# Retention attention with a multiplicative FFN in fp32: order of the first loads, and Strassen products in place of plain ones

## The chip, the cores and the metric

The kernel runs on one NeuronCore of a Trainium2 chip, in a single launch. The metric is the device time of that launch in microseconds (us): 935.48 as the median of nine runs. TensorE (PE) multiplies matrices, VectorE (DVE), ScalarE (ACT) and GpSimd (POOL) work elementwise, and SyncE (SP) issues nearly all the transfers. Each engine works through its own queue in order and meets the others at semaphores.

## The reference

Retention (attention with a decay in place of a softmax) on 8 batches, 8 heads, 576 positions and 64 dimensions gives x, 4608 tokens by 512. Then a feed-forward block multiplies two projections and projects twice:

```python
scores = scale * np.matmul(q, k.transpose(0, 1, 3, 2))
Dmat = np.where(rel >= 0, gamma[:, None, None] ** rel[None, :, :], 0.0)
ret = scores * Dmat[None, :, :, :]
attn = np.matmul(ret, v)
x = attn.transpose(0, 2, 1, 3).reshape(B * S, H * D)
a = x @ w1            # 512 x 1024
b = x @ w2            # 512 x 1024
h = a * b @ w3        # 1024 x 1024
out = h @ w_out       # 1024 x 512
```

q, k, v are float32. The four weights reach the chip as 64-bit floats and are turned into float32 there.

## The kernel before

**Attention.** The batches are taken in four pairs. The 576 positions of a pair are cut into five chunks, the first of 64 and four of 128; a chunk of a pair is called a unit here, so units 0 to 4 are the first pair. For unit g, `load(g, names)` (L95) issues one transfer of 512 KB for each of k, q and v (256 KB for unit 0; two buffers each), `scale` (L158, POOL) multiplies q and v by their decays, `front` (L166) transposes k and q on TensorE with copies on ScalarE, `score` (L183) multiplies them and masks the result into `pm` on VectorE (one buffer), `state` (L199) adds k and v to a running state, and `pv` (L220) multiplies `pm` by v, adds what the state gives, and copies the result into `xT`. A unit's `pv` needs its `score` and the earlier units' `state`.

**Weights.** w1 and w2 are cut into four quarters of columns, `fp` 0 to 3, of four blocks each (512 KB; w1 and w2, two halves of rows), blocks 0 to 15; w_out and w3 follow, 24 blocks more. `load_block` (L261) issues the next block into one of five `raw` buffers; a block whose second index is 1 goes as two transfers. They are numbered raw0, raw1 and so on here. The conversion from 64 bits is a generator: `begin_block` (L295) has three steps on VectorE and two activations on ScalarE, `end_block` (L320) two steps on VectorE, the last writing the block into `wA` and issuing the next load. The order is begin 0, begin 1, end 0, begin 2, end 1 and so on: block n is ended only after block n + 1 was begun. `convert(n)` takes n steps of it at the place where it is called, and `convert_up_to(n)` as many as n blocks need. Nothing reorders these steps later: the order of the calls is the order of the queues.

**Products with w1 and w2.** Tokens of a pair are taken in three parts n of 192 per batch, and `up(i, n, fp)` (L431) multiplies part n of pair i by quarter fp of w1 and w2 with Strassen's scheme: 7 products in place of 8. It needs four sums of each quarter, which `strassen_weights(fp)` (L146) makes from `wA` (S1, S2, S3, S4; S3 in place of a quarter's block), and three sums of tokens T, which `strassen_tokens(i, n)` (L397) makes, the fourth in place in `xT`. The results pass through VectorE additions into a tile `c` (one buffer), and two halves of `c` are multiplied into `ab`. `up_plain` (L413) does the same with 8 products, straight from `wA` and `xT`, with no sums: on TensorE it issues 64 instructions where `up` issues 56. It serves pair 0, part 0, quarters 0 and 1. The order of the start is written out by hand from L501 to L553; behind it, w3 times w_out is folded into one matrix (L563 to L580), and the rest of the kernel alternates attention of the later pairs, `up`, and `down` (L475).

What matters for the order: an engine's instructions stand in its queue as the calls below come. `convert` puts work on VectorE and ScalarE and loads on SP; `front` and `pv` put copies on ScalarE; `score`, `up` and the two `strassen_` functions put work on VectorE.

Of the kernel before, what the change touches and what calls it, by code (L numbers as in the profile page):

```python
# [8 lines left out]
F32 = mybir.dt.float32  # L9
# [23 lines left out]
def kernel(  # L33
# [13 lines left out]
    nc = tc.nc  # L47
# [6 lines left out]
    P = 128  # L54
# [10 lines left out]
    TB = S // NB  # L65
    NT = 2 * TB // P
    KD = DM // P
    KF = DF // P
# [6 lines left out]
    ffn = ctx.enter_context(tc.tile_pool(name="ffn", bufs=2))  # L75
# [12 lines left out]
    acc = ctx.enter_context(tc.tile_pool(name="acc", bufs=7, space=PSUM))  # L88
# [4 lines left out]
    live = {}  # L93

    def load(g, names, engine=nc.sync):  # L95
        i, c = divmod(g, NC)
        sz = sizes[c]
        src = {"k": k, "q": q, "v": v}
        for nm in names:
            t = pools["ld"].tile([P, 2 * H, D], F32, tag="ld_" + nm, name="ld_" + nm)  # L100
            engine.dma_start(  # L101
                t[:sz], src[nm][2 * i:2 * i + 2, :, starts[c]:starts[c] + sz, :].rearrange("b h p d -> p (b h) d"))
            live[nm, g] = t
# [34 lines left out]
    def A(fp, nm):  # L138

        h, m = divmod(fp, 2)  # L140
        if nm in ("S1", "S2", "S4"):
            return wS[h][:, ("S1", "S2", "S4").index(nm), m]
        r, f = {"A11": (0, 0), "A12": (1, 0), "A21": (0, 1), "S3": (0, 1), "A22": (1, 1)}[nm]
        return wA[h][:, :, 2 * r:2 * r + 2, m * QC + f * P:m * QC + f * P + P]

    def strassen_weights(fp):  # L146
        def tt(out, in0, in1, op):
            nc.vector.tensor_tensor(out=A(fp, out), in0=A(fp, in0), in1=A(fp, in1), op=op)  # L148

        tt("S1", "A21", "A22", ALU.add)  # L150
        tt("S2", "S1", "A11", ALU.subtract)
        yield
        tt("S3", "A11", "A21", ALU.subtract)
        tt("S4", "A12", "S2", ALU.subtract)
        live["S", fp] = True
        yield

    def scale(g, nm):  # L158
        c = g % NC
        sz = sizes[c]  # L160
        t, gam = live[nm, g], {"q": gq, "v": gk}[nm]
        t = t[:sz].rearrange("p (b h) d -> p b h d", b=2)
        nc.gpsimd.tensor_tensor(  # L163
            out=t, in0=t, in1=gam[:sz, c].unsqueeze(1).unsqueeze(3).to_broadcast([sz, 2, H, D]), op=ALU.mult)

    def front(g):  # L166
        c = g % NC
        sz = sizes[c]
        kn, qn = live["k", g], live["q", g]
        kT = pools["fr"].tile([P, 2, NP, P], F32, tag="kT", name="kT", bufs=1)  # L170
        qT = pools["fr"].tile([P, 2, NP, P], F32, tag="qT", name="qT")
        for src, dst in ((kn, kT), (qn, qT)):
            for b in range(2):
                tp = acc.tile([P, NP, P], F32, tag="acc", name="tp")
                for p in range(NP):
                    h = b * H + 2 * p
                    nc.tensor.transpose(tp[:, p, :sz],  # L177
                                        src[:sz, h:h + 2, :].rearrange("p a d -> p (a d)"),
                                        ident[:sz, :sz])
                nc.scalar.copy(dst[:, b, :, :sz], tp[:, :, :sz])  # L180
        live["kT", g], live["qT", g] = kT, qT

    def score(g):  # L183
        c = g % NC
        sz = sizes[c]
        kT, qT = live["kT", g], live["qT", g]
        pm = pools["fr"].tile([P, 2, 2, NP, P], F32, tag="pm", name="pm", bufs=1)
        for b in range(2):
            sc = [acc.tile([P, NP, P], F32, tag="acc", name="sc") for j in range(2)]
            for p in range(NP):  # L190
                for j, hs in enumerate(heads):
                    nc.tensor.matmul(sc[j][:sz, p, :sz], kT[hs, b, p, :sz], qT[hs, b, p, :sz],  # L192
                                     start=True, stop=True)
            for j in range(2):
                nc.vector.tensor_mul(pm[:sz, b, j, :, :sz], sc[j][:sz, :, :sz],  # L195
                                     mask[:sz, :sz].unsqueeze(1).to_broadcast([sz, NP, sz]))
        live["pm", g] = pm

    def state(g):  # L199
        c = g % NC  # L200
        sz = sizes[c]
        if c == NC - 1:
            return
        kn, vs = live["k", g], live["v", g]
        if c == 0:
            live["st"] = st_ps.tile([P, 2, NP, D], F32, tag="st", name="st")
        st = live["st"]

        for b in range(2):
            for p in range(NP):  # L210
                for j, hs in enumerate(heads):
                    h = b * H + 2 * p + j
                    nc.tensor.matmul(st[hs, b, p, :], kn[:sz, h, :], vs[:sz, h, :],  # L213
                                     start=(c == 0 and b == 0 and p == 0), stop=(c == NC - 2),
                                     skip_group_check=True)
        sb = pools["fr"].tile([P, 2, NP, D], F32, tag="sb", name="sb")
        nc.scalar.copy(sb, st)
        live["sb", g + 1] = sb
# [101 lines left out]
    def end_block():  # L320
        n = converted[0]
        hi = live["raw", n][:, :, 1]
        e, m = live["em", n]
        vec = nc.vector
        vec.scalar_tensor_tensor(e, in0=hi, scalar=-(1 << 31), in1=e,
                                 op0=ALU.bitwise_and, op1=ALU.bitwise_or)
        yield
        key = blocks[n][0]
        while not (key[0] == "w12" or "wo" in live and (key[0] == "wo" or key[1] < turned[0] + 2)):
            yield "wait"  # L330
        out, m, e = converted_to(n), m.bitcast(F32), e.bitcast(F32)
        if key[0] == "w12":
            m, e = (x.rearrange("p (c n) -> p c n", c=2) for x in (m, e))
        vec.scalar_tensor_tensor(out, in0=m, scalar=2.0 ** -20, in1=e, op0=ALU.mult, op1=ALU.mult)
        converted[0] += 1

        if n > 0:
            load_block()
        if key[0] == "w12" and key[1] > 1 and key[2:] == (1, 1):
            yield from strassen_weights(key[1])  # L340
        yield

# [18 lines left out]
    def convert(n):  # L361

        for _ in range(n):
            if go_on() is not None:
                return

    def convert_up_to(n):
        while converted[0] < n:
            assert go_on() is None
# [40 lines left out]
        minus(B[0][1], B[1][1], B[0][1])  # L410
        minus(T[2], B[1][0], T[1])

    def up_plain(i, n, fp, conv):  # L413

        convert_up_to(4 * (fp + 1))
        if fp == 0:
            live["ab", i, n] = ffn.tile([P, 2 * KF, TB], F32, tag="ab", name="ab")
        ab, x = live["ab", i, n], live["xT", i]
        c = ffn.tile([P, 4, 2, TB], F32, tag="c", name="c", bufs=1)
        for m, (a, b) in enumerate((a, b) for a in range(2) for b in range(2)):  # L420
            ps = acc.tile([P, 2, TB], F32, tag="acc", name="up")
            for w in range(2):
                for r in range(KD):
                    nc.tensor.matmul(ps[:, w, :], A(fp, f"A{a + 1}{r // 2 + 1}")[:, w, r % 2, :],  # L424
                                     x[:, r, b, n * TB:(n + 1) * TB], start=(w == r == 0),
                                     stop=(r == KD - 1), skip_group_check=True)
            nc.scalar.copy(c[:, m, 0], ps[:, 0, :])
            nc.vector.tensor_mul(ab[:, 4 * fp + m, :], ps[:, 1, :], c[:, m, 0])
            convert(conv)

    def up(i, n, fp, conv=0):  # L431
        m = every.index((i, n))
        while ("S", fp) not in live:
# [64 lines left out]
            nc.sync.dma_start(*stores.pop(0))  # L498


    load(1, "kqv")  # L501
    for _ in range(4):
        load_block()
    load(2, "kq")
    load_block()
    scale(0, "q")
    front(0)
    score(0)
    scale(0, "v")
    state(0)  # L510
    scale(1, "q")
    front(1)
    scale(1, "v")
    pv(0)
    load(2, "v")
    state(1)
    convert(3)
    score(1)
    convert(10)
    scale(2, "q")  # L520
    scale(2, "v")
    pv(1)
    load(3, "kq")
    load(3, "v")
    up_plain(0, 0, 0, conv=3)
    front(2)
    state(2)
    score(2)
    convert(5)
    load(4, "kq")  # L530
    scale(3, "q")
    scale(3, "v")
    front(3)
    pv(2)
    load(4, "v")
    state(3)
    score(3)
    up_plain(0, 0, 1, conv=3)
    pv(3)
    for _ in strassen_weights(0):  # L540
        pass
    strassen_tokens(0, 1, nc.vector)
    converting.append(strassen_weights(1))
    scale(4, "q")
    scale(4, "v")
    up(0, 1, 0, conv=2)
    front(4)
    up(0, 1, 1, conv=2)
    score(4)
    strassen_tokens(0, 0, nc.vector)  # L550
    up(0, 0, 2, conv=2)
    pv(4)
    att_part.close()  # L553
# [130 lines left out]
```

## Time and profile before

| | us |
|---|---|
| median of nine runs (lowest, highest) | 935.48 (931.17, 937.22) |
| profiled execution, its own time | 931.17 |
| its span, first to last instruction | 929.4 |
| PE busy | 903.1 (97%) |
| PE weight loads busy | 716.6 (77%) |
| DVE busy | 341.4 (37%) |
| ACT busy | 203.8 (22%) |
| POOL busy | 117.9 (13%) |
| idle of PE ahead of the plain products, 24.47 to 28.38 | 3.91 |
| idle of PE in the plain product, 33.29 to 36.07 | 2.78 |
| idle of PE ahead of the second plain quarter, 62.93 to 64.39 | 1.46 |
| idle of PE in `up(0, 0, 2)`, 102.14 to 106.55 | 4.41 |

The profile is of one execution. Its page cuts the span into 40 slices of 23.2 us, with a digit for the busy tenths of each engine and one for the clock that TensorE was granted. The chain of waits follows the last instruction back to what released it, step by step: each line has a start, a length and what it was. Timeline rows have a start, a length, the engine (with q: its queue, as for issues of transfers), the line, the operation, tiles out and in with their shapes, and in brackets how long the engine sat idle before and what released it. The fp32 products of this kernel show as two matmul instructions each.

### The profile page before, as it was taken

The numbers are of one execution on the slowest core, as the hardware profiler recorded it, in microseconds if no ns is written. First come the engines' busy times: TensorE is split into PE (matmuls) and PEld (weight loads), VectorE is DVE, ScalarE is ACT, GpSimd is POOL, SyncE is SP. The second block draws the span as 40 slices with busy tenths as digits, with TensorE's granted clock in tenths as the row PEclk, the third lists the DMA queues.
The fourth block names the chain that finished last, engine by engine and source line by source line (L and its number), as shares of the span: only waits on it lengthen the run. The fifth ranks groups of instructions, "written<-read, shape, count | busy, mean of one in ns | idle before, by whom it ended". The sixth has DMA issues, their size and how long they took to land.

```text
span 929.4 us, 14132 instructions
## 1 busy us (share of the span) xinstructions
PE 903.1 (97%) x6101; PEld 716.6 (77%) x6101; DVE 341.4 (37%) x593; ACT 203.8 (22%) x377; POOL 117.9 (13%) x87
## 2 busy tenths in 40 slices
PE   6689899999999999999999999999999999999998
PEld 6688799944456779959968959949959959689593
DVE  2679888885001213403313312403313304224040
ACT  3353233345112321111121111111211110011010
POOL 3220020000302423103003020003020101000000
PEclk9799899999999999999999999999999999999999
DMA  9983223342516652303024012134010010000101
GB/s 195 214 195 91 68 71 111 114 127 52 91 49 125 126 110 39 69 23 80 1 48 75 15 46 57 24 68 80 1 46 12 1 35 1 12 23 1 35 1 34
DMA packets 125550, 59.67 MB, mean 64 GB/s; under 512 B 113704, under 2 KB 113704, under 8 KB 125488
## 3 DMA queue, kind: packets, MB, share of 16 engines
q1 hardware_dynamic: 123824, 58.47, 28.2%
q8 instruction: 48, 0.79, 0.4%
q10 hardware_dynamic: 1664, 0.30, 0.2%
q14 instruction: 14, 0.11, 0.0%
HBM read 49.32 MB, written 9.44 MB: 63 GB/s over the span
## 4 chain that ended last, share of the span: by engine, by line
PE 91%; DVE 4%; DMA 2%; SPq 2%; issue 1%; ACT 0%; POOL 0%; DVEq 0%
PE up L448 44%; PE po L479 27%; PE ps L387 6%; PE sc L192 3%; PE xps L241 3%; PE tp L177 3%; SPq L101 2%; PE xps L234 2%; PE up L424 1%; DMA raw<-in_moe_w_dram 1%; PE st L213 1%; DMA ld_v<-in_v_dram 1%; PE tp L377 1%; DVE wS L148 1%; DVE pm L195 1%
## 5 line engine op out<-in xcount | busy, mean ns | idle before, releaser
L453 DVE TENSOR_TENSOR c<-up,c 128x384 f32<-128x384 f32 x230 | 127.9, 556 | 337.6 <-PE up L448 335.9
L479 PE MATMUL po<-w3o,ab 128*128 128x512 f32 x576 | 251.0, 593 | 0.0
L479 PEld LDWEIGHTS po<-w3o,ab 128*128 128x128 f32 x576 | 108.2, 190 | 129.2 <-issue 128.4
L448 PE MATMUL up<-xT,wA 128*128 128x192 f32 x1104 | 204.3, 328 | 0.5 <-ACT xT L245 0.5
L448 PEld LDWEIGHTS up<-xT,wA 128*128 128x128 f32 x1104 | 183.7, 191 | 4.2 <-issue 2.4
L448 PE MATMUL up<-T,wS 128*128 128x192 f32 x736 | 136.6, 329 | 5.3 <-DVE T L404 5.3
L448 PEld LDWEIGHTS up<-T,wS 128*128 128x128 f32 x736 | 123.7, 192 | 5.9 <-issue 4.7
L195 DVE TENSOR_TENSOR pm<-sc,mask 128x512 f32<-128x512 f32 (+1 forms) x80 | 45.4, 628 | 189.6 <-PE sc L192 189.6
L482 ACT COPY ot<-po 128x512 f32<-128x512 f32 x36 | 21.1, 586 | 238.6 <-PE po L479 238.6
L466 ACT COPY c<-up 128x384 f32<-128x384 f32 x46 | 22.0, 478 | 224.9 <-PE up L448 224.8
L163 POOL TENSOR_TENSOR ld_v<-ld_v,gk 128x1024 f32<-128x1024 f32 (+1 forms) x20 | 38.1, 1906 | 257.1 <-DMA ld_v<-in_v_dram 249.8
L163 POOL TENSOR_TENSOR ld_q<-ld_q,gq 128x1024 f32<-128x1024 f32 (+1 forms) x20 | 38.2, 1908 | 245.3 <-DMA ld_q<-in_q_dram 144.6
L448 PE MATMUL up<-xT,wS 128*128 128x192 f32 x368 | 67.7, 327 | 0.2 <-DVE c L453 0.2
L448 PE MATMUL up<-T,wA 128*128 128x192 f32 x368 | 67.3, 326 | 0.0
L448 PEld LDWEIGHTS up<-xT,wS 128*128 128x128 f32 x368 | 60.8, 190 | 1.2 <-DVE c L453 1.1
L448 PEld LDWEIGHTS up<-T,wA 128*128 128x128 f32 x368 | 61.1, 190 | 0.0
L387 PE MATMUL ps<-wo,w3T 128*128 128x512 f32 x128 | 56.3, 592 | 0.0
L472 DVE TENSOR_TENSOR ab<-c 128x768 f32<-128x768 f32 x46 | 44.0, 956 | 3.8
L387 PEld LDWEIGHTS ps<-wo,w3T 128*128 128x128 f32 x128 | 23.7, 190 | 26.8 <-issue 26.8
L459 ACT COPY c<-up 128x384 f32<-128x384 f32 x46 | 22.0, 478 | 84.0 <-DVE ab L472 58.0
L314 ACT ACTIVATE e<-e,lim 128x512 int32<-128x512 int32 x40 | 28.9, 722 | 52.3 <-DVE e L304 52.3
L192 PE MATMUL sc<-qT,kT 64*128 64x128 f32 (+1 forms) x640 | 38.5, 271 | 1.0 <-ACT qT L180 1.0
(55 smaller groups left out, 612.9 us busy)
## 6 DMA issues: line engine op xcount, KB each, us to landing
raw<-in_moe_w_dram SPq DMA_DIRECT2D x24, 512.0 KB, 3.7
ld_k<-in_k_dram SPq DMA_DIRECT2D x16, 512.0 KB, 6.3
ld_q<-in_q_dram SPq DMA_DIRECT2D x16, 512.0 KB, 7.4
ld_v<-in_v_dram SPq DMA_DIRECT2D x16, 512.0 KB, 4.6
out_dram<-ot SPq DMA_DIRECT2D x24, 256.0 KB, 2.0
raw<-in_moe_w_dram SPq DMA_DIRECT2D x16, 256.0 KB, 5.8
raw<-in_moe_w_out_dram SPq DMA_DIRECT2D x8, 512.0 KB, 3.5
out_dram<-ot SPq DMA_DIRECT2D x24, 128.0 KB, 2.3
```

What stands on the lines that cost most here:

```text
L163: nc.gpsimd.tensor_tensor(out=t, in0=t, in1=gam[:sz, c].unsqueeze(1).unsqueeze(3).to_broadcast([sz, 2, H, D]), op=ALU.mult)
L177: nc.tensor.transpose(tp[:, p, :sz], src[:sz, h:h + 2, :].rearrange("p a d -> p (a d)"), ident[:sz, :sz])
L192: nc.tensor.matmul(sc[j][:sz, p, :sz], kT[hs, b, p, :sz], qT[hs, b, p, :sz], start=True, stop=True)
L195: nc.vector.tensor_mul(pm[:sz, b, j, :, :sz], sc[j][:sz, :, :sz], mask[:sz, :sz].unsqueeze(1).to_broadcast([sz, NP, sz]))
L241: nc.tensor.matmul(banks[r][heads[half], b, n, :sz], vs[:sz, b * H + 2 * p + j, :], pm[:sz, b, j, p, :sz], start=(c == 0 and m == 0), stop ...
L314: nc.scalar.activation(e, e, relu, bias=lim[:, 0:1], scale=-1.0)
L387: nc.tensor.matmul(ps, live["w3T", ft][:, g, :], live["wo"][:, g, :], start=(g == 0), stop=(g == KF - 1))
L448: nc.tensor.matmul(ps[:, w, :], a[:, w, r, :], b[:, r, :], start=(new and w == r == 0), stop=(w == r == 1), skip_group_check=True)
L453: nc.vector.tensor_add(c[:, to], ps, c[:, sb])
L459: nc.scalar.copy(c[:, 0], p1)
L472: nc.vector.tensor_mul(ab[:, 4 * fp:4 * fp + 4, :], c[:, :, 0, :], c[:, :, 1, :])
L479: nc.tensor.matmul(po, ab[:, f, t * P:(t + 1) * P], live["w3o"][:, f, :], start=(f == 0), stop=(f == KF - 1))
```

## The change

The order written out by hand at the start of the kernel is another one, and `up_plain` is gone.

- Blocks 0 to 3 are issued ahead of k, q and v of unit 1, block 4 behind them; before, unit 1 went first, and unit 2's k and q between blocks 3 and 4.
- Conversion begins between `front(0)` and `score(0)`; `pv(0)` comes directly after more of it; quarter 0 is converted and its four sums are made ahead of `front(1)`. Blocks 5 to 7 are issued ahead of k, q and v of unit 2.
- `strassen_tokens(0, 0)` comes directly behind `pv(1)` and no longer behind `score(4)`.
- `up(0, 0, 0)` and `up(0, 0, 1)` take the place of the two plain products, the second ahead of `front(2)` and no longer behind `score(3)`.
- The sums of quarter 1 are made as part of its conversion, when its last block is ended, and no longer inside `up(0, 1, 0)`.
- Units 2 and 3 go through `front`, `state`, `score` in a row, and `pv(2)` and `pv(3)` follow; before, `pv(2)` stood ahead of `score(3)`, and `pv(3)` behind the second plain product.

```diff
-        if key[0] == "w12" and key[1] > 1 and key[2:] == (1, 1):
+        if key[0] == "w12" and key[1] > 0 and key[2:] == (1, 1):
             yield from strassen_weights(key[1])
...
-    def up_plain(i, n, fp, conv):
...
-    load(1, "kqv")
     for _ in range(4):
         load_block()
-    load(2, "kq")
+    load(1, "kqv")
     load_block()
     scale(0, "q")
     front(0)
+    convert(3)
     score(0)
     scale(0, "v")
     state(0)
+    convert(5)
+    pv(0)
+    convert_up_to(4)
+    load(2, "kqv")
+    for _ in strassen_weights(0):
+        pass
     scale(1, "q")
     front(1)
     scale(1, "v")
-    pv(0)
-    load(2, "v")
     state(1)
-    convert(3)
     score(1)
-    convert(10)
+    convert(2)
+    pv(1)
+    strassen_tokens(0, 0, nc.vector)
+    load(3, "kqv")
+    up(0, 0, 0, conv=2)
     scale(2, "q")
     scale(2, "v")
-    pv(1)
-    load(3, "kq")
-    load(3, "v")
-    up_plain(0, 0, 0, conv=3)
+    up(0, 0, 1, conv=2)
     front(2)
     state(2)
     score(2)
-    convert(5)
-    load(4, "kq")
+    load(4, "k")
     scale(3, "q")
+    front(3)
     scale(3, "v")
-    front(3)
+    load(4, "q")
+    state(3)
+    score(3)
     pv(2)
     load(4, "v")
-    state(3)
-    score(3)
-    up_plain(0, 0, 1, conv=3)
     pv(3)
-    for _ in strassen_weights(0):
-        pass
     strassen_tokens(0, 1, nc.vector)
-    converting.append(strassen_weights(1))
+    convert(2)
+    up(0, 1, 0, conv=2)
     scale(4, "q")
     scale(4, "v")
-    up(0, 1, 0, conv=2)
     front(4)
     up(0, 1, 1, conv=2)
     score(4)
-    strassen_tokens(0, 0, nc.vector)
     up(0, 0, 2, conv=2)
     pv(4)
     att_part.close()
```

More of the change, by code (lines that the diff above doesn't have):

```diff
@@ L411, in strassen_tokens @@
         minus(T[2], B[1][0], T[1])
-    def up_plain(i, n, fp, conv):
[L415 to L429, printed above, removed]
     def up(i, n, fp, conv=0):
```

## The prediction

> **What bounds the kernel now.** I read the page's slices first, then the chain of waits up to 220 us, then stretches and the timeline of the first 125 us.
>
> ```profile
> PE   6689899999999999999999999999999999999998
> DVE  2679888885001213403313312403313304224040
> PEclk9799899999999999999999999999999999999999
> ```
>
> After slice 5 (116 us) TensorE is full to the end, so everything the change can win or lose lies before that. I follow the run to one mark: the start of `up(0, 1, 2)`, at 120.4 us before (first row of L448 behind the last L241). From there both kernels issue the same work.
>
> ```profile
> 8.24 7.67 DMA ld_v<-in_v_dram
> ...
> 26.56 6.31 DMA raw<-in_moe_w_dram
> ...
> 35.33 0.70 DVE wA L334
> 36.03 0.04 issue
> 36.07 4.36 PE up L424 x13
> ...
> 105.84 0.57 DVE T L404
> 106.41 0.14 issue
> 106.55 11.00 PE up L448 x48
> ```
>
> The chain's transfers end where they land: v of unit 1 at 15.91, the fifth weight block (raw4) at 32.87. Only then can block 3 be finished, since block 4 is begun before block 3 is ended, and the first plain product starts in earnest at 36.07. The last wait is for T at 106.55.
>
> ```profile
> 10.17:13.58 3.41, 3.41 (x64) 3.41 (x64) 1.49 (x4) 0.35 (x1) 0.77 (x1) 1.00 1.34 218
> 13.58:16.99 3.41, 3.41 (x18) 2.93 (x16) 0.00 (x0) 1.92 (x4) 2.91 (x2) 1.00 1.16 270
> ...
> 102.33:105.74 3.41, 0.00 (x0) 0.00 (x0) 3.41 (x7) 1.82 (x3) 0.00 (x0) 1.00 0.35 139
> 105.74:109.15 3.41, 2.60 (x8) 2.63 (x9) 1.56 (x4) 0.00 (x0) 0.00 (x0) 0.50 0.02 5
> 109.15:112.57 3.42, 3.42 (x12) 3.42 (x12) 2.28 (x5) 0.00 (x0) 0.00 (x0) 0.50 0.05 4
> ```
>
> Columns: stretch, length, busy time of PE, PEld, DVE, ACT, POOL, then granted clock, DMA share, GB/s. An idle stretch of 3.41 is followed by half clock, and it takes a fully busy 3.41 to end it. (Before 17 us the clock stands as 1.00 but the rows go at half pace, as the next view shows.)
>
> ```profile
> 13.75 1.97 PE L177 MATMUL tp<-ident,ld_k 128*128 128x128 f32 x8
> ...
> 43.26 1.90 POOL L163 TENSOR_TENSOR ld_q<-ld_q,gq 128x1024 f32<-128x1024 f32 x1 [5.14 <-DMA ld_q<-in_q_dram]
> 43.32 2.38 DVE L334 SCALAR_TENSOR_TENSOR wA<-m,e 128x512 f32<-128x512 f32 x1
> ...
> 46.98 1.04 PE L177 MATMUL tp<-ident,ld_k 128*128 128x128 f32 x8
> ```
>
> Eight transposes take 1.97 at 13.75 and 1.04 at 46.98. And a VectorE operation on two SBUF operands took 2.38 instead of 0.69 when it met a POOL scaling: it waited for the scaling's end.
>
> **What is removed.** Two plain quarters are 2 x 64 matmul instructions, two Strassen ones 2 x 56 (46 such calls make the page's 2576). At 0.164 each (336 in 55.11) the 16 fewer are worth 2.6. On VectorE 8 multiplications of 0.36 become 10 additions of 0.47 and two products of 0.95: 3.7 more, on ScalarE 8 copies of 0.32 become 4 of 0.48; both lie in the walk below. `strassen_tokens(0, 0)` leaves the place behind `score(4)`, so the wait of 4.41 at 102.14 goes, with the half clock behind it (48 instructions in 11.00 against 7.9, so 3.1). Together the old end loses 7.5 of waiting. What is late next there is VectorE's `pm` of 2.48, which TensorE passes with four products in hand.
>
> **What is added, step by step.**
> *SP.* raw0 to raw3 go ahead of k, q, v of unit 1, and raw4 stays behind them. Before, seven transfers of 512 KB lay between 15.91 and 32.87, 2.42 each. Now raw4 lies five (raw0 to raw4) beyond the same start: 15.91 + 5 x 2.42 = 28.0. Bounds by the 253 GB/s of 40 to 50 us (2.07 each) and the 192 of 20 to 30 (2.73): 26.3 to 29.6. Blocks 5 to 7 now pass k, q, v of unit 2; the 18 transfers up to raw8 are the same as before (landing near 52), and it is needed at 59, so this passing costs nothing while that margin of 7 holds. v of unit 3 waits for `pv(1)` and holds SP until 42; raw8 stands behind it, inside the same margin. k, q, v of unit 4 now stand behind raw13 and, for v, behind `pv(2)`: issued by 85 and landed some 6 later, needed by `pv(4)` past 113, so nothing while those 20 hold. POOL keeps its order of scalings.
> *ScalarE and VectorE behind raw4.* `convert_up_to(4)` now stands ahead of `front(1)`. In ScalarE's queue its activations for block 4 hold the copies of kT and qT: landing + 0.55 to the first, 1.45 for two, 3 x 0.59 for the copies to the first qT, so `score(1)` starts at 31.9 (before: 19.48). In VectorE's queue block 4 is begun, block 3 ended (3.15 after landing, rows 32.87 to 36.02) and the four Strassen sums made (2.5, rows 75.25 to 77.77): 33.7; `pm(1)` waits behind them, `pv(1)` behind `pm(1)`, and the first product behind `pv(1)`.
> *The clock at that point.* Between `pv(0)` (15.5) and 31.9 TensorE has only the transposes and `state(1)`. `score(1)` takes 2.06, `pv(1)` 1.10 + 1.97 at full clock, twice that at half. Full throughout: first c addition at 41.0 (pm ends 36.2, L241 1.3 later, then 3.5 to the addition, as 75.86 to 80.63 in the old rows less their T wait). Half throughout: scores end 36.0, L234 38.2, L241 42.1, copy 42.6, two products of 2.6 and 0.4 to the addition: 48.2. Nearest row: 10.17 to 13.58 is TensorE busy without a pause in products on 64 rows, and did not raise the clock; these are products on 64 rows or columns too. I take half, 48.0.
> The Trainium skill (TensorE: Matmul & The Clock Gate, "What's actually happening") gives the clock back after about 3.4 us of sustained activity, whatever the shape. By that rule it would be back near 37, and the sum would be that of the second case below; the stretch at 10.17 speaks against it, and I go by the stretch.
> *From the first addition to the second quarter's S2.* `up(0, 0, 1)` stands directly behind `up(0, 0, 0)`, ahead of `front(2)`, and needs block 6 ended, block 8 begun, block 7 ended, S1 and S2. `up(0, 1, 1)` gives the first part: 93.68 to 102.87, 9.2, and 0.5 as two of its steps are longer kinds here. Then wA 0.7, begin 1.4, 0.65 + 0.7, two sums 1.35: 14.5 in all. The scalings of q and v of unit 3 (landing 47 to 50) fall into it: 0 to 1.69 each, I take 0.7 (half way, as of four such meetings between 31 and 48 us one cost 1.7, one 0.25): 1.4. S2 stands at 48.0 + 15.9 = 63.9.
> *TensorE there.* It ends `up(0, 0, 0)` at 54.4 (42.6 + 56 x 0.164 + 2.6 of half clock), does the one product that needs no S (1.3 to 2.6), and has nothing else: 7 to 8 of waiting, with front, state, score of units 2 and 3 queued behind. Before, just these stood there and covered the conversion. The gap lowers the clock as that of 102.14 did; half clock lasts 3.4 to 6.8 after, so 1.7 to 3.4 lost, I take the middle. End: 63.9 + 7.9 + 2.6 = 74.4.
> *The rest.* Units 2 and 3: 46.82 to 60.71 with its own wait of 1.0 gone, 12.9; `pv(3)` 3.0; 1.1 as `pm(3)` now waits for `pv(2)` (one buffer): 17.0, so 91.4. Then 76.04 to 120.41 less 7.5 and less 1.1 of small T waits: 35.8. The mark: 127.2.
>
> **Sum.** 127.2 - 120.4 = 6.8 longer. The profiled execution took 931.17 (span 929.4), the lowest of the nine; the median is 935.48, and I put the difference on it: 942.3.
>
> **Rivals.** About 0.2% (1.9) is what a measurement of this kernel tells from no change.
> *Clock back during `score(1)`/`pv(1)`* (one full stretch behind 31.9, near 37): L241 ends 39.6, first addition 43.1, S2 59.0, TensorE 69.4, mark 122.2: +1.8, 937.3. For it: 50 to 60 us, the same products, kept a full clock; against: keeping is not raising.
> *The clock never matters* (faster): the full-array transposes of `front(1)` raise it, as 13.58 to 16.99 did, and the gap before S2 doesn't lower it. Addition at 41.0, S2 56.9, end 64.8, mark 117.6: -2.8, 932.7. It decides where both prices, 7.0 and 2.6, are spared; with the first alone it is -0.2. Against it: 3.91 idle at 24.47 lowered the clock at 27.2.
> *Nothing gained or lost*: raw4 at 26.3 and no scaling met, with the clock back near 37: -1.3, 934.2. For it: 270 GB/s at 13.58.
> *Collisions in full*: both scalings at 1.69 and that of v of unit 2 on the token sums, with the clock at half: 6.8 + 2.0 + 1.7 = 10.5, 946.0.
>
> **How the numbers follow.** Forecast 0.47 (own range 938.5 to 945.5), clock back 0.22, clock never matters 0.13, nothing 0.10, collisions 0.08. Slower: 0.47 + 0.11 + 0.08 = 0.66; same: 0.11 + 0.08 = 0.19; faster: 0.13 + 0.02 = 0.15. The range reaches to the fast rival and past the collisions: 932.7 to 947.5.
>
> **What would show it.** Right: `score(1)` near 32, behind the activations of block 4; its 32 products in about 4; the first L453 near 48; TensorE idle some 7 before an `up<-T,wS` near 64, with half clock after; no wait before `up(0, 0, 2)`; the mark near 127. Wrong: raw4 under 26 or over 30; scores in 2.1; TensorE busy over 55 to 64; or a new wait of TensorE behind 91, where I count VectorE as fast enough (some 11 per `up` against 9.2, with two `up` and their scores between).

## The result, and the profile after

| | before | after |
|---|---|---|
| median (lowest, highest), runs | 934.70 (929.84, 937.93), 63 | 937.91 (935.92, 939.97), 21 |
| profiled execution, its own time | 931.17 | 937.34 |
| its span | 929.4 | 935.6 |
| the mark, start of `up(0, 1, 2)` | 120.4 | 125.3 |
| from the mark to the end | 809.0 | 810.3 |

The changed kernel takes 1.0040 times the time of before, with a 95% interval of 1.0029 to 1.0051: 3.7 us more (0.40% of 934.70), slower by more than a measurement's 0.2%. The forecast was 942.3: the sign came true, the size did not.

The slices of the changed kernel's page, to be laid beside those of before:

```profile
PE   4759999999999999999999999999999999999998
...
PEclk9979999999999999999999999999999999999999
```

TensorE's poor slices are now the first three (70 us); the weak spot of before in the fifth slice (93 to 116 us) is gone, and the third has a lowered clock. The chain of waits of the changed kernel (start, length, what) shows where:

```profile
19.97 7.22 DMA raw<-in_moe_w_dram
...
30.72 3.48 PE sc L192 x32
...
41.37 0.54 DVE c L435
...
60.84 9.83 PE up L430 x48
...
125.33 9.31 PE up L430 x56
```

raw4 lands at 27.19, the scores of unit 1 start at 30.72, the first addition into `c` at 41.37, the 48 products behind the second quarter's S2 at 60.84, and the mark is the last row. TensorE's own waits from 34 to 145 us, in total, times, longest, are:

```profile
PE up L430 <- DVE wA L334: 7.4, 1, 7.4
PE up L430 <- DVE c L435: 3.5, 4, 1.1
PE up L430 <- DVE wS L148: 2.8, 1, 2.8
PE up L430 <- DVE T L404: 1.3, 1, 1.3
```

And from 25 to 126 us of before (the products of `up` are L448 there, the plain ones L424):

```profile
PE up L448 <- DVE T L404: 5.3, 2, 4.4
PE up L424 <- DVE wA L334: 4.6, 3, 2.8
PE up L424 <- ACT xT L245: 3.9, 1, 3.9
```

The waits of the plain products have gone, and the 4.4 for T; 1.3 for another T is new. In their place stands one hole of 7.4 + 2.8 in `up(0, 0, 1)`, while VectorE converts the second quarter, as predicted. Three stretches of the changed kernel (stretch, length, then busy time of PE, PEld, DVE, ACT, POOL, clock, DMA share, GB/s) show `score(1)`, the hole and what follows it:

```profile
30.34:33.76 3.42, 3.04 (x28) 3.04 (x30) 3.31 (x6) 1.30 (x3) 0.00 (x0) 1.00 1.16 186
49.02:56.44 7.42, 0.00 (x0) 0.00 (x0) 7.32 (x12) 1.44 (x2) 2.16 (x1) 0.85 0.48 138
...
60.84:70.67 9.83, 9.83 (x50) 9.81 (x51) 6.43 (x13) 2.68 (x5) 0.00 (x0) 0.82 0.16 51
```

The clock column is of use only from 33.76 on, where this trace has its first clock entry; ahead of it the column says 1.00, but the rows go at half pace (eight transposes took 1.97 at 24.88, 1.04 at 70.50). VectorE is busy 7.32 of 7.42 in the hole, TensorE not at all; then 48 products take 9.83 in place of 7.9 at full clock, so 1.9 for the clock. VectorE works without pause, but not at its own pace. From the timeline of the changed kernel (start, length, engine, line, operation):

```profile
38.89 2.14 POOL L163 TENSOR_TENSOR ld_q<-ld_q,gq 128x1024 f32<-128x1024 f32 x1 [11.76 <-DMA ld_q<-in_q_dram]
...
39.19 2.26 DVE L404 TENSOR_TENSOR T<-xT,T 128x384 f32<-128x384 f32 x1
...
41.84 2.31 DVE L311 SCALAR_TENSOR_TENSOR m<-raw,m 128x512 f32<-128x512 uint32 x1
...
46.51 1.90 POOL L163 TENSOR_TENSOR ld_q<-ld_q,gq 128x1024 f32<-128x1024 f32 x1 [2.90 <-DMA ld_q<-in_q_dram]
46.67 2.03 DVE L308 TENSOR_SCALAR m<-raw 128x512 int32<-128x512 int32 x1
...
48.73 0.69 DVE L311 SCALAR_TENSOR_TENSOR m<-raw,m 128x512 f32<-128x512 uint32 x1
48.76 2.42 POOL L163 TENSOR_TENSOR ld_v<-ld_v,gk 128x1024 f32<-128x1024 f32 x1 [0.34 <-DMA ld_v<-in_v_dram]
49.34 0.55 DVE L435 TENSOR_TENSOR c<-up,c 128x384 f32<-128x384 f32 x1
49.80 1.92 DVE L325 SCALAR_TENSOR_TENSOR e<-raw,e 128x512 int32<-128x512 int32 x1
```

The steps at 46.67 and 49.80 took 2.03 and 1.92 in place of 0.42 and 0.68, each ending 0.3 to 0.6 behind the POOL scaling (L163) that ran beside it; an L311 at 41.84 took 2.31 in place of 0.69 beside an earlier scaling. The three are 4.5 us more. A fourth, the token sum at 39.19, took 2.26 in place of 0.56 just ahead of the first addition. That is the question for the first part of the study: how much of the 3.7 is such meetings of a VectorE step with a POOL scaling, and how much the hole itself? Below, each run has its median (lowest to highest) and its ratio to before with a 95% interval; two changed kernels are compared by their ratios, times 934.7.

### The profile page after: what moved, and what is told of

It reads as the page before. It is cut to its first block, busy times and chain, and to the rows that moved or that the text cites. A ratio compares the mean times of both kernels' runs of the same rounds, so it can differ in the third digit from the quotient of the medians.

```text
span 935.6 us, 14109 instructions
## 1 busy us (share of the span) xinstructions
PE 899.3 (96%) x6085; PEld 712.6 (76%) x6085; DVE 355.5 (38%) x597; ACT 202.5 (22%) x373; POOL 119.0 (13%) x87
## 4 chain that ended last, share of the span: by engine, by line
PE 90%; DVE 5%; DMA 2%; issue 2%; ACT 1%; SPq 1%; ACTq 0%; DVEq 0%
PE up L430 43%; PE po L461 27%; PE ps L387 6%; PE sc L192 4%; PE xps L241 4%; PE tp L177 3%; PE xps L234 2%; PE st L213 2%; DVE c L435 1%; SPq L101 1%; DMA gk<-decay_k_dram 1%; DMA raw<-in_moe_w_dram 1%; DVE e L325 1%; PE tp L377 1%; DVE T L404 1%
## 5 line engine op out<-in xcount | busy, mean ns | idle before, releaser
L435 DVE TENSOR_TENSOR c<-up,c 128x384 f32<-128x384 f32 x240 | 133.4, 556 | 338.6 <-PE up L430 333.9
L430 PE MATMUL up<-xT,wA 128*128 128x192 f32 x1152 | 213.4, 328 | 8.3 <-DVE wA L334 7.4
L430 PEld LDWEIGHTS up<-xT,wA 128*128 128x128 f32 x1152 | 191.5, 191 | 12.6 <-DVE wA L334 7.7
L430 PE MATMUL up<-T,wS 128*128 128x192 f32 x768 | 142.0, 328 | 4.0 <-DVE wS L148 2.8
L430 PEld LDWEIGHTS up<-T,wS 128*128 128x128 f32 x768 | 128.4, 191 | 4.8 <-issue 4.8
L430 PE MATMUL up<-xT,wS 128*128 128x192 f32 x384 | 70.8, 327 | 3.6 <-DVE c L435 3.5
L163 POOL TENSOR_TENSOR ld_q<-ld_q,gq 128x1024 f32<-128x1024 f32 (+1 forms) x20 | 38.4, 1922 | 273.2 <-DMA ld_q<-in_q_dram 265.8
L448 ACT COPY c<-up 128x384 f32<-128x384 f32 x48 | 23.0, 478 | 225.4 <-PE up L430 222.6
L163 POOL TENSOR_TENSOR ld_v<-ld_v,gk 128x1024 f32<-128x1024 f32 (+1 forms) x20 | 39.1, 1955 | 253.2 <-DMA ld_v<-in_v_dram 253.2
L430 PE MATMUL up<-T,wA 128*128 128x192 f32 x384 | 70.2, 326 | 0.0
L430 PEld LDWEIGHTS up<-xT,wS 128*128 128x128 f32 x384 | 63.4, 190 | 5.0 <-DVE c L435 5.0
L430 PEld LDWEIGHTS up<-T,wA 128*128 128x128 f32 x384 | 63.7, 190 | 0.0
L454 DVE TENSOR_TENSOR ab<-c 128x768 f32<-128x768 f32 x48 | 46.6, 970 | 3.8
```

What stands on the lines that cost most here:

```text
L163: nc.gpsimd.tensor_tensor(out=t, in0=t, in1=gam[:sz, c].unsqueeze(1).unsqueeze(3).to_broadcast([sz, 2, H, D]), op=ALU.mult)
L430: nc.tensor.matmul(ps[:, w, :], a[:, w, r, :], b[:, r, :], start=(new and w == r == 0), stop=(w == r == 1), skip_group_check=True)
L435: nc.vector.tensor_add(c[:, to], ps, c[:, sb])
L454: nc.vector.tensor_mul(ab[:, 4 * fp:4 * fp + 4, :], c[:, :, 0, :], c[:, :, 1, :])
```

## Experiments

**1. Before once more.** The kernel before, unchanged, to see how its executions differ.

> The kernel before, unchanged, for a second profiled execution. The first one took 931.17, the lowest of its nine, and the prediction put a difference worked out on that execution onto the median. Theory P (the profiled execution was a favourable one): this one is nearer to 935, and some wait ahead of 120 us is longer in it, the plain product's waits for block 3 or 7, the wait for T at 102, or the half clock behind one of them; the start of up(0, 1, 2) stands 2 to 5 us later than 120.4. Rival Q (the difference lies in what the rest of the kernel or the launch takes): the start of up(0, 1, 2) is within 1 us of 120.4 whatever the time is.

936.47 (931.36 to 937.74), ratio 1.0013 (0.9993 to 1.0032). The second profiled execution took 936.48, 5.3 more than the first, and its mark lies at 125.7 in place of 120.4: all 5.3 lie ahead of the mark. Its timeline shows one of the places:

```profile
64.55 2.13 POOL L163 TENSOR_TENSOR ld_v<-ld_v,gk 128x1024 f32<-128x1024 f32 x1 [0.78 <-DMA ld_v<-in_v_dram]
...
64.95 2.27 DVE L334 SCALAR_TENSOR_TENSOR wA<-m,e 128x512 f32<-128x512 f32 x1
```

Its longest waits from 25 to 126 us, and a stretch behind that write (columns as above):

```profile
PE up L424 <- DVE wA L334: 9.0, 3, 3.6
```

```profile
66.24:73.07 6.83, 5.79 (x18) 5.79 (x19) 2.71 (x5) 1.76 (x3) 0.44 (x1) 0.50 0.25 77
```

Here four writes of `wA` (at 31.52, 35.96, 45.35 and 64.95) met a scaling and took 2.27 to 2.31, TensorE waited 9.0 for `wA` in place of 4.6, and the last of these waits brought half clock over 66.24 to 73.07. So the time of before depends on which instructions happen to meet, and its first profiled execution, 3.5 below the median of 63 runs, was one that met few. These are two executions; experiment 5 takes the scalings away.

**2. The hole filled.** Units 2 and 3 go ahead of `up(0, 0, 1)`, so that TensorE has work while quarter 1 is converted; `pv(2)` comes ahead of `score(3)` again, and the loads of unit 4 move with it.

```diff
     scale(2, "q")
     scale(2, "v")
-    up(0, 0, 1, conv=2)
     front(2)
     state(2)
     score(2)
-    load(4, "k")
+    convert(4)
+    load(4, "kq")
     scale(3, "q")
+    scale(3, "v")
     front(3)
-    scale(3, "v")
-    load(4, "q")
+    pv(2)
+    load(4, "v")
+    convert(3)
     state(3)
     score(3)
-    pv(2)
-    load(4, "v")
+    up(0, 0, 1, conv=2)
     pv(3)
```

> The changed kernel with up(0, 0, 1) moved back behind score(3), so that front, state and score of units 2 and 3 and pv(2) (some 14 us of TensorE) stand in the place where it waited 7.4 and 2.8 us; the rest of quarter 1's conversion and its sums stand between them. Theory W (the time is lost in that wait, because nothing else was queued there): TensorE reaches the end of pv(3) some 10 us sooner than at 87, the half clock after 54 is gone, and the whole is 8 to 13 us faster than the changed kernel, so 925 to 930 and faster than the kernel before. Rival V (VectorE is the bound of the start: it is busy 97 of the first 125 us, against 84 of 120 before): the wait only moves behind 87, to the additions into c, and the whole gains under 3 us: 935 or more.

930.00 (927.64 to 931.06), ratio 0.9955 (0.9939 to 0.9970): 7.9 less than after, just short of the 8 to 13 that were expected, and faster than before. Its waits from 34 to 145 us, and ScalarE's timeline:

```profile
PE sc L192 <- ACT qT L180: 5.5, 2, 5.0
```

```profile
54.07 0.72 ACT L315 ACTIVATE e<-e,lim 128x512 int32<-128x512 int32 x1
...
55.64 1.08 ACT L180 COPY qT<-tp 128x512 f32<-128x512 f32 x2
```

The hole of 7.4 + 2.8 is gone. In its place `score(2)` waits 5.0, since its copies of kT and qT stand in ScalarE's queue behind the activations of block 7, and these behind VectorE's first conversion step. Half clock stayed with it: the 32 products of `score(2)` took 3.79, 2.06 at full clock. The order of the calls, not the amount of work, makes the hole.

**3. No scalings in the hole.** The changed kernel without the four scalings of units 2 and 3.

```diff
-    scale(2, "q")
-    scale(2, "v")
...
-    scale(3, "q")
...
-    scale(3, "v")
```

> The changed kernel without the decays of q and v of units 2 and 3 (four POOL operations of 1.9 us are left out, and with them a part of the computation). In the changed kernel five VectorE operations between 39 and 52 us took 1.9 to 2.3 instead of 0.4 to 0.7 beside them. Theory C (VectorE stood still behind POOL and that is on the path to S2 of quarter 1): S2 is ready near 55.5 to 56.5 instead of 60.7, and the whole is 4 to 5 us faster than the changed kernel, about 933.5. Rival D (VectorE waits there for TensorE or a transfer in any case): S2 is under 1.5 us earlier, and the whole gains under 1.5.

932.99 (931.71 to 934.60), ratio 0.9995 (0.9980 to 1.0009): 4.2 less than after. Its waits from 34 to 145 us:

```profile
PE up L430 <- DVE wA L334: 3.6, 1, 3.6
PE up L430 <- DVE wS L148: 3.5, 1, 3.5
```

The two waits of the hole shrink from 10.2 to 7.1. From the first addition (42.29) to the end of S2 (57.14) it takes 14.9, where the working had 14.5 without any meeting and the changed kernel needs 19.3. S2 stands at 57.14, behind the 55.5 to 56.5 that were expected, since the first addition came 0.9 later than in the changed kernel. (Between 39 and 52 us its rows show four steps of 1.9 to 2.3, those named above, not five.) The rest of the hole stays: it is VectorE's own work.

**4. The clock held up.** The changed kernel with products that nobody reads where TensorE waits: 22 ahead of `up(0, 0, 1)`, 8 behind its first product.

```diff
+        if (i, n, fp) == (0, 0, 1):
+            warm(8)
...
+    warm(22)
     up(0, 0, 1, conv=2)
```

> The changed kernel with 22 extra products, read by nobody, in TensorE's wait ahead of up(0, 0, 1), and 8 more behind its first product: 7.2 and 2.6 us of work in waits of 7.4 and 2.8. Theory H (the wait costs its length and, behind it, half clock): the clock stays at 1.00 over 54 to 64 us, the 48 instructions behind the wait take 7.9 instead of 9.8, and the whole is 1.5 to 2.5 us faster than the changed kernel, about 935.9. Rival N (the half clock is hidden, since VectorE's additions and sums pace those products): the 48 instructions are faster, but the whole gains under 0.5.

936.20 (934.80 to 937.38), ratio 1.0025 (1.0009 to 1.0041): 1.4 less than after, where 1.5 to 2.5 were expected; the two intervals overlap, so the time alone is weak evidence. Its stretch over the place of the hole:

```profile
49.00:56.40 7.40, 7.40 (x46) 7.40 (x47) 7.30 (x12) 2.71 (x5) 1.18 (x1) 1.00 0.50 124
```

The clock stays at 1.00, here and from 56.4 to 64, and the gain does not contradict the 1.9 read from the 48 products; the hole itself remains.

**5. Both kernels without the later scalings.** Before and after, each without the six scalings of units 2, 3 and 4; those of units 0 and 1 stay.

```diff
-    scale(2, "q")
-    scale(2, "v")
...
-    scale(3, "q")
-    scale(3, "v")
...
-    scale(4, "q")
-    scale(4, "v")
```

Of before:

> The kernel before without the decays of q and v of units 2, 3 and 4 (six POOL operations are left out, and with them a part of the computation). Two profiled executions of the kernel before differ by 5.3 us, all of it ahead of up(0, 1, 2): in the slower one four VectorE operations that write wA took 2.27 instead of 0.69 beside a scaling, in the faster one a single one did. Theory S (what differs from execution to execution is which VectorE operation meets a scaling): median 929 to 931, lowest and highest within 3 us of each other where the kernel before has 7 to 8. Rival T (it is the transfers' arrival or the phase of the clock's windows): the spread stays above 5 us and the median within 2 us of 934.5.

Of the changed kernel:

> The changed kernel with the same six operations left out. Against the run without the first four of them (932.99) only the two of unit 4 are gone, one of which held the token sums at 88 us by 1.5. Theory S: 931 to 932, and the difference to the kernel before without the six, 1 to 3 us, is what the order alone costs, without collisions. Rival U (the change loses its time by meeting more scalings than before): with the six gone the changed kernel is equal to the kernel before without them within 0.7 us, or faster.

Before: 929.92 (928.38 to 933.41), ratio 0.9952 (0.9933 to 0.9970). After: 931.25 (930.22 to 932.81), ratio 0.9962 (0.9946 to 0.9979). From the mark to the end, first of before, then of the changed kernel:

```profile
119.38:928.40 809.02, 805.47 (x5146) 625.96 (x5144) 258.27 (x437) 157.39 (x296) 97.59 (x70) 1.00 0.23 51
```

```profile
119.60:929.90 810.30, 805.68 (x5146) 625.94 (x5144) 258.60 (x436) 157.07 (x296) 97.60 (x70) 1.00 0.22 51
```

Without the scalings the marks lie at 119.4 and 119.6, a tie, and the medians 1.3 apart, which is what the stretch behind the mark shows (810.30 against 809.02). The marks are of one profiled execution each, but both lie within 0.5 of their medians (930.13 and 931.71). So the exchange of the old waits for the hole is about an even one by itself. The scalings cost before 0.48% (4.5 us) and the changed kernel 0.78% (7.3), each with an interval of some 2 us, so the gap between the two costs is less sure than the tie of the marks. Before spread over 5.0 without them (6.4 in the twelve runs of experiment 1), not the 3 or less that was expected, though eleven of the twelve runs lie within 2.9; what makes the rest of the spread is open.

**6. The token sums alone.** Before, with `strassen_tokens(0, 0)` taken from its late place to one ahead of `up(0, 1, 1)`, as the one part of the change that removes a wait.

```diff
     front(4)
+    strassen_tokens(0, 0, nc.vector)
     up(0, 1, 1, conv=2)
     score(4)
-    strassen_tokens(0, 0, nc.vector)
     up(0, 0, 2, conv=2)
```

> The kernel before with one part of the change alone: strassen_tokens(0, 0) stands ahead of up(0, 1, 1) and no longer behind score(4). The prediction held that the old end loses 7.5 us, 4.4 of waiting for T at 102 and 3.1 of half clock behind it. Theory E (they are gained, less what VectorE is then late by, some 2.4 at the additions of up(0, 0, 2)): 4 to 6 us faster than the kernel before, 929 to 931. Rival V (VectorE is the bound there, so that the four sums cost as much where they are put): under 2 us faster.

930.91 (926.73 to 933.42), ratio 0.9960 (0.9941 to 0.9979): 3.7 less than before, just under the 4 to 6 of theory E and well over the 2 of its rival. The wait for T of 4.4 is gone with its half clock, and a small one, for an addition into `c`, takes its place (waits of TensorE, 25 to 145 us):

```profile
PE up L448 <- DVE c L453: 2.7, 3, 2.1
```

This part of the change is a gain, and can be had without the rest.

**7. The loads alone.** Before, with the first loads in the changed order and nothing else.

```diff
-    load(1, "kqv")
     for _ in range(4):
         load_block()
-    load(2, "kq")
+    load(1, "kqv")
     load_block()
+    load(2, "kq")
```

> The kernel before with the order of the first loads alone: raw0 to raw3 ahead of k, q, v of unit 1, raw4 behind them and ahead of k and q of unit 2. Theory W (the first plain product waits for raw4 through block 3): raw4 lands near 27.2 instead of 32.9, unit 1's pv near 31, the product begins in earnest at 31 to 33 instead of 36 to 38, and 2 to 4 us of that are left at the end: 931 to 933. Rival L (what unit 1 loses at the start, some 8 us of its transfers, and the later waits for blocks 6 and 7 and the collisions take it back): within 1 us of 934.5.

940.66 (938.58 to 944.01), ratio 1.0068 (1.0047 to 1.0089): 6.4 slower, and neither theory had that. Its timeline:

```profile
30.06 2.48 DVE L195 TENSOR_TENSOR pm<-sc,mask 128x512 f32<-128x512 f32 x4 [15.88 <-PE sc L192]
...
45.66 0.59 PE L424 MATMUL up<-xT,wA 128*128 128x192 f32 x2 [1.89 <-DVE wA L334]
```

Earlier weights are of no use in the old order of calls. In ScalarE's queue the first activations of a block (29.12) stand behind unit 1's copies, in VectorE's the end of block 0 behind `pm(1)`, and VectorE stood idle for 15.88 ahead of that. With unit 1 arriving later, its `pv` moves into the conversion, and the plain product starts in earnest at 45.66, not 36.07. The change needs its moves of `convert` and of `pv(0)` to bear its loads.

**8. The hole filled, with ScalarE ahead.** As in 2, but `up(0, 0, 0)` takes one conversion step fewer between its products, and four steps stand behind `state(2)`, so that unit 2's copies come ahead of block 7's activations.

```diff
-    up(0, 0, 0, conv=2)
+    up(0, 0, 0, conv=1)
...
     front(2)
     state(2)
+    convert(4)
     score(2)
-    convert(4)
+    convert(6)
     load(4, "kq")
```

> The changed kernel with units 2 and 3 ahead of up(0, 0, 1), as in the run at 930.0, and half of the conversion steps of up(0, 0, 0) moved behind front(2) and score(2). In that run TensorE still waited 5.0 us ahead of score(2), because the copies of qT stood in ScalarE's queue behind activations that waited for VectorE's begin of block 7. Theory A (the ScalarE queue makes that wait): the wait is under 1.5, no half clock follows, and the whole is 926 to 928. Rival V (VectorE is the bound, and the wait moves to the masks of unit 2 or to S2): 929 to 931.

926.06 (925.04 to 927.58), ratio 0.9907 (0.9877 to 0.9936): 8.7 less than before. Of the wait of 5.0 ahead of `score(2)` 1.34 are left, under the 1.5 that was expected; but 2.02 now stand ahead of `score(3)`, at 62.58, and half clock follows them (63.57 to 66.98), which was not expected. Both are in this line (waits from 34 to 145 us):

```profile
PE sc L192 <- ACT qT L180: 3.4, 2, 2.0
```

**9. Two conversion steps fewer at the mark.** The changed kernel without the `convert(2)` ahead of `up(0, 1, 0)`. In the changed kernel TensorE waits 1.0 in `up(0, 0, 3)`, behind the mark, for an addition into `c` that stands behind a conversion step of VectorE (L334 from 141.94 to 142.95). The timeline:

```profile
142.88 0.55 DVE L435 TENSOR_TENSOR c<-up,c 128x384 f32<-128x384 f32 x1
...
143.48 1.57 PE L430 MATMUL up<-xT,wS 128*128 128x192 f32 x8 [1.04 <-DVE c L435]
```

```diff
     strassen_tokens(0, 1, nc.vector)
-    convert(2)
     up(0, 1, 0, conv=2)
```

> The changed kernel without the convert(2) ahead of up(0, 1, 0), so that later conversion steps stand where they stand in the kernel before. In all runs of the changed order so far, the time from the start of up(0, 1, 2) to the end is 810.4, in those of the old order 809.0, and TensorE waits 1.05 for an addition into c in up(0, 0, 3), between whose additions the changed kernel has two long conversion steps beside POOL's token sums, the old one a short and a long one. Theory F (those two steps, two positions further on, make the wait): it is gone, the rest takes 809.1 to 809.5, and the whole is 1.0 to 1.4 us faster than the changed kernel, about 936.7. Rival V (VectorE is simply later in the changed order): the wait stays within 0.3 of 1.05, and the rest at 810.3.

935.38 (934.51 to 936.57), ratio 1.0016 (1.0001 to 1.0031): 2.2 less than after, more than the 1.0 to 1.4 expected. Its stretch from the mark:

```profile
125.28:934.60 809.32, 805.67 (x5146) 625.73 (x5144) 258.95 (x438) 157.69 (x296) 98.29 (x70) 1.00 0.22 51
```

Behind the mark it is back at 809.3, and three of the four waits for `c` ahead of 145 us are gone (3.5 in four became one of 1.1). Where the further 1.2 comes from is not settled: the profiled execution (936.28, above the median) has its mark at 125.3 like the changed kernel's.

**10. Both together.** Kernel 8 without that `convert(2)`.

> The run at 926.06 (units 2 and 3 ahead of up(0, 0, 1), half of the conversion of up(0, 0, 0) behind front(2)) without that convert(2) too. Theory F: 1.0 to 1.4 us faster than that run, 924.7 to 925.1, and clear of the kernel before by 9 us. Rival V: 926 as before.

923.47 (921.79 to 923.77), ratio 0.9876 (0.9859 to 0.9893): 11.6 less than before, 15.3 less than the change as given, over five runs. That is 2.9 less than kernel 8, more than the 1.0 to 1.4 that were expected. Its mark lies at 112.7 (115.5 in kernel 8), the rest at 809.3 (810.4), its longest wait from 34 to 145 us is 1.4, and no half clock comes behind 35.9 until the end. Why the mark moved too is as open as in experiment 9.

## Why the prediction came out as it did

**The step that failed most: the difference put on the median.** Between the two profiled executions the working said 6.8, and 6.2 came (937.34 less 931.17). But it was put on the median of before, and the profiled execution of before lay 3.5 below the 934.70 that more runs gave, that of after only 0.6 below its own. Of the 4.4 between 942.3 and 937.91, that is 3.0; 0.8 is the median of nine runs against that of 63, 0.6 the sum itself, and that the sum is so near is luck, as the terms below show. Experiment 1 shows what the text had not asked: whether the rows it summed (waits for `wA` of 4.6, one meeting of 1.7 and one of 0.25) were those of a usual execution. In the second one they were 9.0 and four meetings.

**Loads.** Said: raw4 at 28.0, scores at 31.9 (the terms given add up to 31.8), behind block 4's activations. Measured: 27.19 and 30.72, behind those activations. Right, 1.2 early. That the load order is no gain by itself, experiment 7 shows. The reverse, the new order of calls with the old loads, no run tried.

**The clock in `score(1)`: wrong.** "Half throughout" put the first addition at 48.0. The scores took 3.48 in place of the 4.1, the clock stood at 1.00 from 33.76, and the addition came at 41.37. Less the 1.2 of the earlier start, "full throughout" had 39.8 and "clock back" 41.9. So the addition was 6.6 early: 1.2 by the start and some 6.2 by the clock, while the token sum at 39.19, which stands ahead of it on VectorE, gave back some 0.8 (the addition came 4.41 behind the start of the copies at 36.96, and 3.63 in experiment 2, where no token sum met a scaling). Here the Trainium skill (TensorE: Matmul & The Clock Gate, "What's actually happening"), with its 3.4 us or so of sustained activity, was nearer than the stretch at 10.17 that I set against it. A "fully busy 3.41" was too strict as well: one stretch of 3.42, in which products on 64 rows kept TensorE busy for 3.04, was enough. The two stretches differ in the shape of their products (64 by 64 at 10.17); no run tried whether that is the reason.

This execution was a favourable one here. Eight profiles have the changed order up to this point, and in them the clock came back for good at 33.55 to 37.16, in five of them at 35.90 or later, as "clock back" had it (near 37). In experiment 3 the scores had kept TensorE busy for 2.77 of the 3.41 from 30.34 and the clock came back only one stretch later. Where these stretches lie differs from execution to execution, and with it the price of this step; none of the eight went at half throughout.

**Meetings with POOL: mis-sized.** From the first addition to S2 I had 14.5, and 1.4 for two scalings. The 14.5 is borne out by experiment 3 (14.9). The meetings were three, 4.5 in sum, about the 4.4 between 19.3 and 14.9. The conversion, 6.6 earlier than said, met v of unit 2 as well as q and v of unit 3, and they cost 1.6, 1.6 and 1.2, not 0.7 each. S2 came at 60.7, not 63.9.

**The hole.** Said 7 to 8 of waiting and 1.7 to 3.4 of clock; measured 7.42 + 2.75 and 1.9 (9.83 against 7.9). The mechanism was right, the length short by the meetings: in experiment 3 it is 7.1. The end of the 48 products: 70.67 for 74.4. Units 2 and 3: 16.4 for 17.0, right.

**From there to the mark.** Said 35.8, measured 38.3. The wait of 4.4 and its half clock went, as said; experiment 6 has that part alone at 3.7 of the 7.5 that the rows of the first profile gave it, with a new wait of 2.1. But new waits of 1.3 (T, held by the scaling of v of unit 4), 0.8 and 0.6 (additions into `c`) came, near the "new wait of TensorE behind 91" named as what would be wrong.

**"From there both kernels issue the same work": wrong by 1.3.** It is the same work on TensorE, but the conversion is two steps further on, and a step now stands ahead of an addition that TensorE waits for. Experiment 9 took 1.0 of the 1.3 back; the other 0.3 is open.

So errors of both signs cancelled, by luck: 6.6 up to the first addition, 0.5 from S2 to the end of the 48 products and 0.6 in units 2 and 3 were too much; 3.4 from the first addition to S2, 2.5 to the mark and 1.3 behind it were too little. Of the rivals, "clock back" had the mechanism; that its 937.3 is near the 937.91 is luck too, since its mark (122.2) is 3.1 early and its 1.8 is put on the same median. "Clock never matters" fell, since the hole did lower the clock (0.82 over the 48 products), though its first addition, 41.0, was near. The rival "collisions in full" was right that the scalings are met nearly in full, and the token sums too, beside the wrong clock.

In sum the change is slower by 3.7 as follows. Its hole, 7.1 without the later scalings, uses up what the removed waits had given: without those scalings the marks tie (experiment 5). The stretch behind the mark adds 1.3. The remaining 2.4 lie ahead of the mark and come with the scalings, which now meet a conversion that TensorE stands waiting for; that scalings cost the changed kernel 4.2 there, experiment 3 shows, but the 2.4 is a difference of differences, about as large as its uncertainty.

## What to carry to other kernels

Before a difference is worked out from one profiled execution, ask where that execution lies among the runs, and which rows in it (here waits behind VectorE steps that may or may not meet POOL) would be others in the next. When products are moved ahead of independent work, look at what that work had covered: the steps of the conversion are the same in both orders, and putting the attention of units 2 and 3 back over it made 8.7 us of gain out of 3.7 of loss, once the copies that the scores need stood ahead of the activations in ScalarE's queue. A count of background steps called between products is a phase for all that follows: two steps more cost 1.0 us far behind their place, and without them the two kernels took 2.2 and 2.9 less.

## What the runs showed of the hardware

A VectorE step that reads only SBUF and starts under a POOL scaling is held until the scaling is over (2.31 for 0.69, 2.03 for 0.42, 1.92 for 0.68). In the thirteen kept traces 51 such steps began under a scaling of q or v that had 0.4 us or more to go, and all ended 0.28 to 0.55 behind its end. One that takes an operand from PSUM is not: the addition into `c` at 49.34 took 0.55 beside a scaling that ran from 48.76 to 51.18. The step that began at 48.73, just ahead of that scaling, took its usual 0.69, and the scaling 2.42 in place of 1.90. The Trainium skill (GPSIMD Engine Reference, "1. Specifications") names the interfaces that the two engines share, and instructions with two SBUF inputs among those that contend. The runs show the size to be the remainder of the POOL instruction, and the step at 46.67, with one SBUF input, to be held too. Which steps meet differs from execution to execution; it is a part of what spreads the runs of before (6.4 us in the twelve of experiment 1, 5.0 in twelve without the later scalings).

The clock came back within a stretch of 3.42 that was busy for 3.04 (30.34 to 33.76), where one of before with 2.60 of 3.41 had not brought it back (105.74 to 109.15), nor had 2.77 in experiment 3 (30.34 to 33.75) and 2.69 in experiment 9 (29.60 to 33.02). The share is not all of it: 3.41 of 3.41 in 64-by-64 products did not bring it back either (10.17 to 13.58 of before).
